# Attention and two feed-forward layers on one core: row factors applied to the softmax weights, not to the values and the output

## The chip, the cores and the metric

The kernel runs on one core of one Trainium2 chip. The metric is the device time of one execution in microseconds (us); smaller is better. Engines are named as in the profile: PE (TensorE, the matrix multiplier; PEld is its weight load), DVE (VectorE), ACT (ScalarE), POOL (GpSimd) and SP (SyncE, which here only issues DMA transfers).

## The reference, cut to what matters

```python
# B=4, H=8, S=576, D=64; all float32
scores = q @ k.T / sqrt(D); scores = where(causal, -1e9, scores)
a = exp(scores - scores.max(-1)); a /= a.sum(-1) + 1e-9
local = a @ v
q_p = phi(q)                       # where(q > 0, q, exp(q) - 1) + 1
mem_out = (q_p @ M_prev) / (q_p . z_prev + 1e-6)
g = 1 / (1 + exp(-beta))           # one number per head
attn = g * mem_out + (1 - g) * local
x = attn as (B*S, H*D)             # 2304 tokens of 512
x = (s * relu(x @ w_in)**2 + b) @ w_out          # d_ff = 2048
out = P(x @ w2_in) / Q(x @ w2_in) @ w2_out       # cubic over quadratic, d_ff = 2048
```

The weights of the two feed-forward layers come as 64-bit floats and are decoded on the chip into a high and a low part; the products are made of three matmuls each.

## The kernel before, in words

**Order of work.** All operations are first listed with their buffers, a cost for each engine that could do them (`ways`) and a due time; a list scheduler (`Plan.run`) then fixes the engine of each operation and the order on every engine, and the engines run these queues in order. Every plain load and store is issued by SP through one line, L364, in one in-order queue. A buffer that is reused comes from a ring (`at_ring(name, role, n, ...)`); a new user of a place waits for all users of the one before. RQ, RP, RT, RU and RV are the ring lengths of the queries and keys, the softmax weights, their transposes, one special transpose, and the values (`vm`).

**Attention.** There are 32 units: for each of 4 batches first the low rows (queries 0 to 383) and then the high rows (384 to 575), and in each of these four pairs of heads. A unit goes through these functions:

- `prepare_qk`, `prepare`: loads. Transposed queries `q` and keys `k` come as one transfer each and head (four a unit), values and the memory matrix as `vm` (ring of RV = 1), untransposed queries as `qm`.
- `scores`, `scores_last` (L610 to L679): score matmuls (L636, L670), masked row minimum on DVE (L643, L673), exponential on ACT (L654, L677) into the weight tiles `p` and `pu`, with row sums into `rs`.
- `sums` (L681): adds 1e-9 to `rs` (L690) and writes the reciprocals into `rec` (L693). For all but the first four units ("direct"), `rec` is then transposed on PE (L700, tile `ct`), copied to `c1`, written to DRAM (`crow`), and read back as a tile `cb` in which each row's reciprocal stands along the free axis of all 64 partitions of its head.
- `phi_a`, `phi_b`: the feature map of the queries, scaled by gate and norm (`c2`) and, in L721, by the row sum, so that the later multiplication by `cb` takes it out again; then transposed into `fs` (and `fl`). In the first four units `phi_b` also builds `cb`, by an expansion of `rec` into `rb`, three transposes and a copy.
- `split_v` (L587): the values of both heads times 1 - g (`omg`), into `vs`, two operations a unit, on whichever of ACT, DVE and POOL the scheduler picks.
- `transposes`, `transposes_last`: the weight tiles are transposed on PE (L504, L819) and copied into `th`.
- `values` (L832): products of `vs` and `th` (L848) and of the memory and `fs` (L856) into one PSUM tile `av`; DVE multiplies it by `cb` into `xp` (L859), which is stored.

**Around it.** While the units run, SP also loads the packed weights of the first half of layer one (tiles `dA...`), DVE, ACT and POOL decode them, and PE works on three narrow blocks of that half (`ha` L904, `acc` L977). When attention is done its memory is given to the second half's weights; wide blocks follow (`hw` and `aw`, then `hb`, `ab`, `hc`, `ac`).

Of the kernel before, what the change touches and what calls it, by code (L numbers as in the profile page):

```python
# [29 lines left out]
RQ, RP, RT, RU, RV = 3, 7, 8, 1, 1  # L30
# [224 lines left out]
def tile_kernel(ctx, tc, qk, vm, z, beta, w1i, w1o, s1, b1, w2i, w2o, a2, b2, out):  # L255
# [76 lines left out]
    cst.tile([P, 40], F32, name="fill_c")  # L332
# [4 lines left out]
    for n in ("rec0", "rec1", "qd0", "qd1"):  # L337
        plan.bufs[n].const = True
# [167 lines left out]
    def prepare_qk(p):  # L506
        u = units[p]
        r = u.r
        src = qk[u.b, u.hp].rearrange("p (j s) -> p j s", j=2)
        at_ring(f"q{p}", "q", RQ, [P, r.nq])  # L510
        at_ring(f"k{p}", "k", RQ, [P, r.nk])
        for j in range(2):
            m = slice(j * D, j * D + D)
            load(lambda m=m: g(f"q{p}")[m], lambda j=j, m=m: src[m, j, r.q0:r.q0 + r.nq], D * 4 * r.nq, (), ((f"q{p}", j),))
            load(lambda m=m: g(f"k{p}")[m], lambda j=j, m=m: src[m, j, SQ:SQ + r.nk], D * 4 * r.nk, (), ((f"k{p}", j),), p < 2)

    def diagonal(p):

        Q, QD = f"q{p}", f"qd{p % 2}"
# [67 lines left out]
    def split_v(p):  # L587

        hp, kb = units[p].hp, units[p].r.kb
        V, VS = f"vm{p}", f"vs{p}"  # L590
        at_ring(VS, "vs", 2, [P, kb, 2, D])
        for j in range(2):
            o = omg[:, 2 * hp + j:2 * hp + j + 1]

            def fn(e, j=j, o=o):
                src = g(V)[:, 0:kb].rearrange("p j (h d) -> p j h d", h=2)[:, :, j]
                if e is nc.scalar:
                    e.activation(g(VS)[:, :, j], src, AF.Copy, scale=o)
                else:
                    e.tensor_scalar(g(VS)[:, :, j], src, o, 0.0, ALU.mult, ALU.add)  # L600

            op(ways(kb * D, 0.09, 0.5, 0.5), fn, (V, "omg"), ((VS, j),), port=True)
# [7 lines left out]
    def scores(p):  # L610

        r = units[p].r
        Q, K, RS = f"q{p}", f"k{p}", f"rs{p}"
# [4 lines left out]
        for i, (cols, pieces) in enumerate(r.scores):  # L618
# [6 lines left out]
            for t, x, ka, kb, o in pieces:  # L625
# [55 lines left out]
    def sums(p):  # L681

        r = units[p].r
        RS, REC = f"rs{p}", f"rec{p % 2}"
        if r.tb == 4:
# [16 lines left out]
        copy(lambda: g(C1), lambda: g(CT)[0:nr, 0:P], P, (CT,), (C1,), act=-0.04)
        crow = dram.tile([2, r.nqt], F32, name=f"crow{p}")
        CR = f"crow{p}"
        buf(CR, None, obj=crow)
        if r.tb < NQ - 1:
            load(lambda: crow.rearrange("j (t q) -> (j t) q", q=P), lambda: g(C1), 1e4, (C1,), ((CR, 0),))
        else:
            load(lambda: crow[:, 0:P], lambda: g(C1)[0:2], 1e4, (C1,), ((CR, 0),))
            load(lambda: crow[:, P:P + 64].unsqueeze(0), lambda: g(C1)[2:3].rearrange("o (j q) -> o j q", j=2), 1e4, (C1,), ((CR, 1),))  # L710
        for j in range(2):
            load(lambda j=j: g(CB)[64 * j:64 * j + 64], lambda j=j: crow[j:j + 1, 0:r.nq].to_broadcast([64, r.nq]),
                 64 * 4 * r.nq, (CR,), ((CB, j),), late=LANDS_CB)

    def phi_b(p):

        r = units[p].r
        F, C, FS, PT, C1, CB, REC = (f"{x}{p}" for x in ("ph", "c2_", "fs", "pf", "c1_", "cb", "rec"))
        REC = f"rec{p % 2}"
        RS = f"rs{p}"  # L720
        small(lambda e: e.tensor_tensor(g(C), g(C), g(RS)[:, :, r.ta:r.tb + 1], ALU.mult), (RS, C), (C,))  # L721
# [6 lines left out]
        here = not r.direct or 2 * w <= 512
        RB = f"rb{p}"
        if r.direct:  # L730
            at_ring(RB, "xp", 2, [P, r.nt, P])
            copy(lambda: g(RB).rearrange("p t (h d) -> p h t d", h=2),
                 lambda: g(REC)[:, 0:2 * r.nt].rearrange("p (h t) -> p h t", h=2).unsqueeze(3).to_broadcast([P, 2, r.nt, D]),
                 r.nt * P, (REC,), (RB,), dve=0.5, pool=0.41)
# [11 lines left out]
        def along(dst, o1):  # L746

            for j in range(r.ta, r.tb + 1):
                flip(dst(), o1 + q0s[j] - r.q0, g(RB)[:, j - r.ta], j)

        def tr():
            phi_t()
            if r.direct and here:
                along(lambda: g(PT), w)

        pe(2 * r.nqt * (2 if r.direct and here else 1), tr, (F, RB) if r.direct and here else (F,), (PT,))
        if not r.direct:
            pass
        elif here:
            copy(lambda: g(CB), lambda: g(PT)[:, w:2 * w], w, (PT,), (CB,), act=-0.04)  # L760
        else:
            CT = f"ct{p}"
            bank(CT, free_banks(p))
            pe(2 * r.nqt, lambda: along(lambda: g(CT), 0), (RB,), (CT,))
            copy(lambda: g(CB), lambda: g(CT)[:, 0:w], w, (CT,), (CB,), act=-0.04)
# [66 lines left out]
    def values(p, runs):  # L832
# [3 lines left out]
        VS, FS, XP, AV, CB = (f"{x}{p}" for x in ("vs", "fs", "xp", "av", "cb"))  # L836
# [14 lines left out]
        pe(2 * sum(x[6] - x[5] for x in part) + 50 * len(part), mm, sorted({x[3] for x in part}) + [VS], (AV,))  # L851
# [7 lines left out]
        op(ways(w, None, 1.0), lambda e: e.tensor_tensor(g(XP), g(AV)[:, 0:w], g(CB), ALU.mult), (AV, CB), (XP,))  # L859
# [322 lines left out]
    for p in range(NPR):  # L1182
# [8 lines left out]
        events.append((t + 0.2, lambda p=p: split_v(p)))  # L1191
# [178 lines left out]
```

## Time and profile before

| | |
|---|---|
| median of 3 runs | 1040.17 us (1039.48 to 1042.01) |
| profiled execution, its own time | 1042.3 us |
| span of its instructions | 1040.5 us |
| PE, DVE, ACT, POOL busy, share of the span | 97%, 82%, 64%, 42% |
| mean granted TensorE clock | 0.988 of full speed |

A row of the view of stretches gives, for each stretch of time, the busy microseconds and the instructions of each engine, the granted clock of PE as a share of full speed, and the busy share of the DMA engines. The chain that ended last is followed back from the last instruction, at each step to what released it. In a row of the page or of a group, "dst<-src" are tile names without their numbers; a releaser is what ended an idle time.

### The profile page before, as it was taken

What the parts mean: (1) busy time and instruction counts of PE and PEld (TensorE: products, weight loads), DVE (VectorE), ACT (ScalarE), POOL (GpSimd) and SP (SyncE); (2) the same over time, 40 slices, a digit from 0 to 9 for tenths busy, and PEclk for the clock granted to TensorE, in tenths of its full rate; (3) what the DMA queues carried; (4) which work ended last, traced back from release to release, by engine and by line L of the source; (5) the groups of instructions that cost most, each with busy time, mean ns of one, the idle gap of its engine ahead of it and who ended that gap; (6) DMA issues with size and microseconds to landing.
All of it is one profiled execution on the core that took longest, in us unless ns stands there. A gap on an engine that the chain in (4) does not pass through costs nothing.

```text
span 1040.5 us, 16335 instructions
## 1 busy us (share of the span) xinstructions
PE 1008.0 (97%) x5396; PEld 835.2 (80%) x5396; DVE 854.5 (82%) x1470; ACT 668.9 (64%) x1415; POOL 439.3 (42%) x507
## 2 busy tenths in 40 slices
PE   6979989999999999999999999999999999999998
PEld 4557677887788886878878999888888888899997
DVE  6989889788849998999996444988888888888896
ACT  6967779677644544544444234777877776877886
POOL 3435433112101211212020004877776867867785
PEclk9989999999999999999999999999999999999999
DMA  6765676655423546676661235700100200100000
GB/s 190 229 206 168 191 229 208 175 162 151 117 61 126 181 139 227 209 243 196 226 211 37 89 102 149 246 0 21 59 1 1 72 1 1 36 28 1 31 1 31
DMA packets 76789, 123.58 MB, mean 119 GB/s; under 512 B 11832, under 2 KB 44704, under 8 KB 76704
## 3 DMA queue, kind: packets, MB, share of 16 engines
q1 hardware_dynamic: 72016, 113.74, 35.4%
q0 software_dynamic: 4224, 8.39, 2.6%
q8 instruction: 43, 0.70, 0.3%
q10 hardware_dynamic: 464, 0.40, 0.2%
q14 instruction: 42, 0.34, 0.1%
HBM read 95.17 MB, written 27.32 MB: 118 GB/s over the span
## 4 chain that ended last, share of the span: by engine, by line
PE 72%; DVE 13%; DMA 7%; ACT 4%; issue 2%; SPq 1%; POOL 0%; ACTq 0%; DVEq 0%; POOLq 0%
PE hc L904 19%; PE ac L1139 19%; PE ab L1053 5%; PE hb L904 5%; PE hw L904 5%; PE aw L1016 4%; PE av L848 3%; PE ha L904 3%; PE s L636 3%; PE acc L977 2%; PE pt L504 2%; ACT p L654 1%; SPq L364 1%; DMA vm<-in_vm 1%; DMA k<-in_qk 1%
## 5 line engine op out<-in xcount | busy, mean ns | idle before, releaser
L1118 DVE RECIPROCAL qe<-qe 128x512 f32<-128x512 f32 (+2 forms) x82 | 242.6, 2959 | 49.2 <-POOL qe L380 49.2
L904 PE MATMUL hc<-xc_h,w2ih 128*128 128x512 f32 (+1 forms) x320 | 117.9, 368 | 0.0
L904 PE MATMUL hc<-xc_h,w2il 128*128 128x512 f32 (+1 forms) x320 | 117.8, 368 | 0.0
L904 PE MATMUL hc<-xc_l,w2ih 128*128 128x512 f32 (+1 forms) x320 | 117.7, 368 | 0.0
L380 POOL TENSOR_TENSOR qe<-qe,qb 128x512 f32<-128x512 f32 (+2 forms) x82 | 94.9, 1157 | 52.5 <-ACT qb L1103 51.4
L1139 PE MATMUL ac<-w2oh,ghc 128*128 128x512 f32 x288 | 112.6, 391 | 0.0
L1139 PE MATMUL ac<-w2ol,ghc 128*128 128x512 f32 x288 | 112.5, 391 | 0.0
L1139 PE MATMUL ac<-w2oh,glc 128*128 128x512 f32 x288 | 112.3, 390 | 0.0
L380 POOL TENSOR_TENSOR glc<-po,ghc 128x512 fp32r<-128x512 f32 (+2 forms) x82 | 95.0, 1158 | 23.3 <-ACT ghc L370 23.1
L380 POOL TENSOR_TENSOR pm<-pm,s 128x512 f32<-128x512 f32 (+2 forms) x82 | 95.6, 1166 | 18.7 <-ACT pm L1103 17.8
L1109 ACT ACTIVATE s<-hc 128x512 f32<-128x512 f32 (+2 forms) x82 | 44.7, 546 | 63.1 <-PE hc L904 60.2
L654 ACT ACTIVATE p<-s,st 128x128 f32<-128x128 f32 (+3 forms) x128 | 66.9, 531 | 19.1 <-DVE st L643 17.9
L1103 ACT ACTIVATE pm<-hc,prm 128x512 f32<-128x512 f32 (+2 forms) x82 | 59.7, 727 | 24.4 <-DVE hc L1120 24.0
L504 PE MATMUL pt<-ident,p 128*128 128x128 f32 x320 | 58.6, 280 | 9.6 <-ACT th L370 4.8
L904 PEld LDWEIGHTS hc<-xc_h,w2il 128*128 128x128 f32 x320 | 60.1, 188 | 8.8 <-DVE po L1122 0.3
L904 PEld LDWEIGHTS hc<-xc_l,w2ih 128*128 128x128 f32 x320 | 60.1, 188 | 8.6
L904 PEld LDWEIGHTS hc<-xc_h,w2ih 128*128 128x128 f32 x320 | 60.1, 188 | 7.6
L1103 ACT ACTIVATE qb<-s,cq,b1abs 128x512 f32<-128x512 f32 (+2 forms) x82 | 62.7, 764 | 2.1 <-POOL qe L380 2.1
L643 DVE CUSTOM_DVE_ANT_0 s<-s,mask 128x128 f32<-128x128 f32 (+3 forms) x128 | 60.5, 508 | 4.3 <-PE s L636 2.9
L1139 PEld LDWEIGHTS ac<-w2oh,ghc 128*128 128x128 f32 x288 | 54.0, 188 | 11.4
L1139 PEld LDWEIGHTS ac<-w2oh,glc 128*128 128x128 f32 x288 | 54.1, 188 | 11.0 <-POOL glc L380 0.6
L1139 PEld LDWEIGHTS ac<-w2ol,ghc 128*128 128x128 f32 x288 | 54.1, 188 | 10.5
(488 smaller groups left out, 2844.1 us busy)
## 6 DMA issues: line engine op xcount, KB each, us to landing
vm<-in_vm SPq DMA_DIRECT2D x16, 384.0 KB
k<-in_qk SPq DMA_DIRECT2D x32, 144.0 KB
out_y<-ob SPq DMA_DIRECT2D x18, 256.0 KB
qm<-in_vm SPq DMA_DIRECT2D x16, 256.0 KB
w2d<-sh SPq DMA_DIRECT2D x16, 256.0 KB
w2d<-sl SPq DMA_DIRECT2D x16, 256.0 KB
w2oh<-w2d POOLq DMA_DIRECT2D x4, 1024.0 KB, 16.9
w2ol<-w2d POOLq DMA_DIRECT2D x4, 1024.0 KB, 18.5
```

The costliest lines, as they stand in the source:

```text
L380: op(ways(c, None, dve, pool), lambda e: e.tensor_tensor(dst(), x(), y(), alu), r, w, port=True)
L504: nc.tensor.transpose(dst[:, o:o + P], src, ident)
L636: nc.tensor.matmul(g(b)[:, o2:o2 + kb - ka], g(Q)[m, q], g(K)[m, ka:kb], start=True, stop=True)
L643: e.tensor_tensor_reduce(sp, sp, mask[:, m0:m0 + kb - ka], -scale, 3.0e38 if x == 0 else st[:, t:t + 1], ALU.add, ALU.min, st[:, t + x:t + ...
L654: e.activation(g(f"p{n}_{i}")[:, o:o + kb - ka], g(b)[:, o2:o2 + kb - ka], AF.Exp, scale=-1.0, bias=g(f"st{n}")[:, z_:z_ + 1], accum_out=g ...
L904: nc.tensor.matmul(hs(), m, y, start=c == 0 and k == 0, stop=c == KC - 1 and k == 2)
L1016: nc.tensor.matmul(g(ACC)[:, 0:w], outp(y, f)[:, cs], g(z_), start=f == 0 and k == 0, stop=f == HF - 1 and k == 2)
L1053: nc.tensor.matmul(g(ACC)[:, 0:w], outp(y, f)[:, cs], g(z_), start=f == 0 and k == 0, stop=f == HF - 1 and k == 2)
L1103: return lambda e: e.activation(g(dst)[:, ks], g(src)[:, ks], AF.Identity, scale=m, bias=b)
L1109: op(ways(c, -0.04), lambda e, ks=ks: e.activation(g(S2)[:, ks], g(HS)[:, ks], AF.Square), (HS,), part(S2))
L1118: op({"DVE": 0.07 + c * 0.00625}, lambda e, ks=ks: e.reciprocal(g(QE)[:, ks], g(QE)[:, ks]), part(QE), part(QE))
L1139: nc.tensor.matmul(g(ACC), g(x_)[:, ks], g(f"w2o{y}{i}")[:, o], start=f == 0 and q == 0, stop=f == NF - 1 and q == 2)
```

## The change: what it does

The row factor (1 - g) / (sum + 1e-9) is computed in place in `rs`, and each weight tile is multiplied by it, row block by row block, before it is transposed: a new helper `scaled` in `sums`, six operations in a low unit and three in a high one, each on ACT, DVE or POOL. The values are used straight from `vm`; `vs`, `rec`, `ct`, `c1`, `crow`, `cb` and `rb` go, with L721. `xp` becomes a copy that ACT or DVE can make. Queries and keys of a head come in one transfer into one tile `qk`; in the high units this takes the 64 columns between them along. RP goes from 7 to 9 and RV from 1 to 3. `gates` makes a small table `omg2` for the high units, three more short DVE copies.

```diff
-RQ, RP, RT, RU, RV = 3, 7, 8, 1, 1
+RQ, RP, RT, RU, RV = 3, 9, 8, 1, 3
...
-        at_ring(f"q{p}", "q", RQ, [P, r.nq])
-        at_ring(f"k{p}", "k", RQ, [P, r.nk])
+        w = r.ko + r.nk
+        at_ring(f"qk{p}", "q", RQ, [P, w])
         for j in range(2):
             m = slice(j * D, j * D + D)
-            load(lambda m=m: g(f"q{p}")[m], ... ((f"q{p}", j),))
-            load(lambda m=m: g(f"k{p}")[m], ... ((f"k{p}", j),), p < 2)
+            load(dst, rows_, D * 4 * w, (), ((f"qk{p}", j),), p < 2 and j == 1)
...
-    def split_v(p):
-        at_ring(VS, "vs", 2, [P, kb, 2, D])
-        for j in range(2):
-            ...
-            op(ways(kb * D, 0.09, 0.5, 0.5), fn, (V, "omg"), ((VS, j),), port=True)
+    def split_m(p):
...
-        small(lambda e: e.reciprocal(g(REC)[:, 0:2 * r.nt].rearrange(by, h=2), g(RS)[:, :, ts]),
-              (RS,), (REC,), ("DVE",))
-        if r.direct:
-            return
-        pe(2 * P, lambda: nc.tensor.transpose(g(CT)[:, 0:P], g(REC), ident), (REC,), (CT,))
-        copy(lambda: g(C1), lambda: g(CT)[0:nr, 0:P], P, (CT,), (C1,), act=-0.04)
-        ... one or two loads C1 -> crow, two loads crow -> CB
+        small(lambda e: e.reciprocal(g(RS)[:, :, ts], g(RS)[:, :, ts]), (RS,), (RS,), ("DVE",))
+        small(lambda e: e.tensor_tensor(
+            g(RS)[:, :, ts], g(RS)[:, :, ts], omg2[:, 2 * hp:2 * hp + 2] if r.tb == 4
+            else omg[:, 2 * hp:2 * hp + 2].unsqueeze(2).to_broadcast([P, 2, r.nt]), ALU.mult), (RS, "omg", "omg2"), (RS,))
+
+        def scaled(name, part, a, b, c):
+            def fn(e):
+                x = g(name)[:, a:b]
+                if e is nc.scalar:
+                    e.activation(x, x, AF.Copy, scale=g(RS)[:, c[0], c[1]:c[1] + 1])
+                else:
+                    e.tensor_scalar(x, x, g(RS)[:, c[0], c[1]:c[1] + 1], 0.0, ALU.mult, ALU.add)
+
+            op(ways(b - a, 0.09, 0.5, 0.41), fn, ((name, part) if part is not None else name, RS),
+               ((name, part) if part is not None else name,), port=True)
+
+        for i, (cols, pieces) in enumerate(r.scores):
+            for t, x, ka, kb, o in pieces:
+                for j in range(2):
+                    scaled(f"p{2 * p + j}_{i}", t, o, o + kb - ka, (j, t))
+        if r.tb == 4:
+            scaled(f"pu{p}", None, 0, S, (0, 4))
...
-        small(lambda e: e.tensor_tensor(g(C), g(C), g(RS)[:, :, r.ta:r.tb + 1], ALU.mult), (RS, C), (C,))
...
-            copy(lambda: g(RB)..., lambda: g(REC)..., r.nt * P, (REC,), (RB,), dve=0.5, pool=0.41)
-            pe(2 * r.nqt, lambda: along(lambda: g(CT), 0), (RB,), (CT,))
-            copy(lambda: g(CB), lambda: g(CT)[:, 0:w], w, (CT,), (CB,), act=-0.04)
...
-                nc.tensor.matmul(g(AV)[64 * j:64 * j + 64, ra:rb], g(VS)[:, kb, j], g(TH)[:, o:o + rb - ra],
+                nc.tensor.matmul(g(AV)[64 * j:64 * j + 64, ra:rb], g(V)[:, kb, D * j:D * j + D], g(TH)[:, o:o + rb - ra],
...
-        op(ways(w, None, 1.0), lambda e: e.tensor_tensor(g(XP), g(AV)[:, 0:w], g(CB), ALU.mult), (AV, CB), (XP,))
+        copy(lambda: g(XP), lambda: g(AV)[:, 0:w], w, (AV,), (XP,), act=-0.04)
```

## Rows read from the trace of the kernel before

**Rows 1.** Stretches of the span: busy us of PE, PEld, DVE, ACT, POOL; clock, DMA.
```profile
0.00:16.00 16.00, 7.50 (x38) 6.13 (x38) 7.75 (x39) 6.96 (x22) 3.97 (x17) 1.00 0.68 212
16.00:160.00 144.00, 129.64 (x877) 93.65 (x878) 128.25 (x393) 113.24 (x329) 59.58 (x115) 0.93 0.69 202
60.00:80.00 20.00, 14.93 (x83) 10.35 (x85) 15.16 (x51) 13.15 (x42) 7.88 (x15) 0.69 0.69 211
160.00:304.00 144.00, 142.66 (x1114) 115.19 (x1115) 116.05 (x389) 99.86 (x292) 30.28 (x76) 1.00 0.52 150
304.00:1040.00 736.00, 728.16 (x3373) 620.20 (x3368) 602.46 (x652) 448.86 (x774) 345.44 (x299) 1.00 0.29 95
```

**Rows 2.** The chain that ended last, 0 to 160 us, shares by line.
```profile
by line: DMA vm<-in_vm 6.6%; DMA k<-in_qk 6.6%; SPq L364 6.0%; DMA qm<-in_vm 5.1%; PE s L636 5.0%; ACT p L654 4.9%; DMA q<-in_qk 4.7%; PE pt L504 3.9%; PE av L848 3.7%; PE ha L904 3.5%; DVE s L643 3.4%; issue 3.3%; DMA dAo2r<-in_w1o 3.3%; D
```

**Rows 3.** The same chain, 160 to 304 us.
```profile
by line: PE acc L977 15.4%; PE av L848 15.1%; PE ha L904 14.9%; PE s L636 12.6%; PE pt L504 11.5%; PE su L670 5.7%; PE av L856 5.6%; ACT p L654 3.8%; PE pf L504 2.6%; PE pt L819 2.3%; PE ct L700 1.6%; DVE s L643 1.4%; DMA qm<-in_vm 1.3%; is
```

**Rows 4.** Pieces of the chain in order of time: start, length, what.
```profile
70.50 5.83 DMA vm<-in_vm
...
81.86 1.81 PE ha L904 x15
...
104.63 0.33 PE pf L504 x3
```

**Rows 5.** DMA issues on SP's queue (L364) up to 305 us: min/median/max ns of an issue.
```profile
L364 SPq DMA_DIRECT2D q<-in_qk x64: 465/549/1625, 0.7 to 264.5; - x64
L364 SPq DMA_DIRECT2D k<-in_qk x60: 465/588/1107, 4.6 to 267.1; - x60
L364 SPq DMA_DIRECT2D cb<-crow x56: 444/588/2330, 51.6 to 303.6; - x56
L364 SPq DMA_DIRECT2D crow<-c x44: 244/302/661, 47.1 to 299.9; - x44
```

**Rows 6.** Waits of POOL up to 305 us: total, times, longest.
```profile
POOL vs L600 <- DMA vm<-in_vm: 43.2, 12, 9.4
```

**Rows 7.** Operations that go: engine, operation, count: min/median/max ns.
```profile
L600 POOL TENSOR_SCALAR vs<-vm,omg x23: 425/495/897, 9.2 to 233.6; 128x192 f32<-128x192 f32 x14, 128x320 f32<-128x320 f32 x9
L600 DVE TENSOR_SCALAR vs<-vm,omg x17: 339/419/1051, 9.1 to 290.1; 128x320 f32<-128x320 f32 x9, 128x192 f32<-128x192 f32 x8
L598 ACT ACTIVATE vs<-vm,omg x24: 442/560/564, 23.8 to 290.1; 128x320 f32<-128x320 f32 x14, 128x192 f32<-128x192 f32 x10
L370 ACT COPY c<-ct x15: 238/250/256, 49.2 to 299.3; 4x128 f32<-4x128 f32 x8, 6x128 f32<-6x128 f32 x7
```

**Rows 8.** Groups by shape up to 305 us: busy us, mean ns; idle before.
```profile
L572 DVE TENSOR_SCALAR qm<-qm 128x384 f32<-128x384 f32 x5 | 1.8, 360 | 0.5 <-ACT ph L566 0.3
L572 DVE TENSOR_SCALAR qm<-qm 128x256 f32<-128x256 f32 x3 | 0.9, 288 | 0.0
L570 ACT ACTIVATE qm<-qm,ones 128x384 f32<-128x384 f32 x3 | 1.9, 633 | 0.0
L570 ACT ACTIVATE qm<-qm,ones 128x256 f32<-128x256 f32 x7 | 3.6, 518 | 0.1
L574 POOL TENSOR_SCALAR qm<-qm 128x384 f32<-128x384 f32 x8 | 4.1, 511 | 10.9 <-ACT ph L566 8.3 <-issue 1.7 <-DMA xTd<-xp 0.7
L574 POOL TENSOR_SCALAR qm<-qm 128x256 f32<-128x256 f32 x6 | 2.4, 405 | 15.5 <-ACT ph L566 6.5 <-DMA qm<-in_vm 5.1 <-DMA q<-in_qk 3.7
L859 DVE TENSOR_TENSOR xp<-av,cb 128x384 f32<-128x384 f32 x16 | 8.8, 549 | 0.7 <-PE pt L504 0.6
L370 ACT COPY th<-pt 128x384 f32<-128x384 f32 x98 | 44.5, 489 | 3.1 <-PE pt L504 3.0
```

**Rows 9.** The transposes of the reciprocals on PE, and the first unit's start.
```profile
L700 PE MATMUL ct<-ident,rec 128*128 128x128 f32 x28 | 8.4, 300 | 0.6 <-ACT p L654 0.3 <-ACT th L370 0.3
...
11.09 1.02 PE L504 MATMUL pt<-ident,p 128*128 128x128 f32 x6 [0.27 <-POOL qm L574]
...
14.34 0.17 DVE L690 TENSOR_SCALAR rs<-rs 128x6 f32<-128x6 f32 x1
```

More of the change, by code (lines that the diff above doesn't have):

```diff
@@ L308, in tile_kernel @@
         nc.gpsimd.affine_select(m, m, pattern=[[-1, 64]], compare_op=ALU.is_ge, fill=-2.0e9 / scale, base=0, channel_multiplier=1)
-    for n in ("rec0", "rec1", "qd0", "qd1"):
+    for n in ("qd0", "qd1"):
         t = at.tile([P, P], F32, name=n)
@@ L331, in tile_kernel @@
     omg = cst.tile([P, H], F32, name="omg")
-    cst.tile([P, 40], F32, name="fill_c")
+    omg2 = cst.tile([P, H, 2], F32, name="omg2")
+    buf("omg2", None, obj=omg2)
+    cst.tile([P, 24], F32, name="fill_c")
     buf("gate", None, obj=gate)
@@ L336, in tile_kernel @@
     buf("sb", None, obj=sb)
-    for n in ("rec0", "rec1", "qd0", "qd1"):
+    for n in ("qd0", "qd1"):
         plan.bufs[n].const = True
@@ L398, in gates @@
         op(ways(H, None, 1.0), lambda e: e.tensor_copy(gate2[:, :, 0], gate), ("gate",), (("gate2", 0),))
+        op(ways(H, None, 1.0), lambda e: e.tensor_copy(omg2[:, :, 0], omg), ("omg",), (("omg2", 0),))
+        for j in range(2):
+            m = slice(64 * j, 64 * j + 64)
+            op(ways(H, None, 1.0), lambda e, j=j, m=m: e.tensor_copy(
+                omg2[m, :, 1].rearrange("p (a h) -> p a h", h=2), omg[m, j::2].unsqueeze(2).to_broadcast([64, NP, 2])),
+               ("omg",), (("omg2", 1 + j),))
         for j in range(2):
@@ L478, in tile_kernel @@
         r.nqt = r.nt * P
+        r.ko = r.nk if r.ta == 0 else SQ - r.q0
         r.where = {t: (i, o) for i, (_, pieces) in enumerate(r.scores) for t, x, _, _, o in pieces if x == 0}
@@ L509, in prepare_qk, with dst, rows_ @@
         src = qk[u.b, u.hp].rearrange("p (j s) -> p j s", j=2)
-        at_ring(f"q{p}", "q", RQ, [P, r.nq])
-        at_ring(f"k{p}", "k", RQ, [P, r.nk])
+        w = r.ko + r.nk
+        at_ring(f"qk{p}", "q", RQ, [P, w])
         for j in range(2):
             m = slice(j * D, j * D + D)
-            load(lambda m=m: g(f"q{p}")[m], lambda j=j, m=m: src[m, j, r.q0:r.q0 + r.nq], D * 4 * r.nq, (), ((f"q{p}", j),))
-            load(lambda m=m: g(f"k{p}")[m], lambda j=j, m=m: src[m, j, SQ:SQ + r.nk], D * 4 * r.nk, (), ((f"k{p}", j),), p < 2)
+            def dst(m=m):
+                return g(f"qk{p}")[m].rearrange("p (x s) -> p x s", x=2) if r.ta == 0 else g(f"qk{p}")[m]
+            def rows_(m=m, j=j):
+                if r.ta:
+                    return src[m, j, r.q0:r.q0 + w]
+                two = qk[u.b, u.hp][m, (2 * S if j else 0):(2 * S if j else 0) + 2 * SQ].rearrange("p (x s) -> p x s", x=2)
+                o = j * (SQ - S)
+                return two[:, :, o:o + r.nk]
+            load(dst, rows_, D * 4 * w, (), ((f"qk{p}", j),), p < 2 and j == 1)
     def diagonal(p):
-        Q, QD = f"q{p}", f"qd{p % 2}"
+        Q, QD = f"qk{p}", f"qd{p % 2}"
         for j in range(2):
@@ L585, in phi_a @@
             if units[p].r.tb < NQ - 1 else gate2[:, 2 * hp:2 * hp + 2], ALU.mult), (C, "gate", "gate2"), (C,))
-    def split_v(p):
-        hp, kb = units[p].hp, units[p].r.kb
-        V, VS = f"vm{p}", f"vs{p}"
-        at_ring(VS, "vs", 2, [P, kb, 2, D])
-        for j in range(2):
[L593 to L600, printed above, removed]
-            op(ways(kb * D, 0.09, 0.5, 0.5), fn, (V, "omg"), ((VS, j),), port=True)
+    def split_m(p):
         if units[p].r.split_m:
@@ L612, in scores @@
         r = units[p].r
-        Q, K, RS = f"q{p}", f"k{p}", f"rs{p}"
+        QK, RS = f"qk{p}", f"rs{p}"
         ns = (2 * p, 2 * p + 1)
@@ L635, in mm @@
                         m = slice(D * j, D * j + D)
-                        nc.tensor.matmul(g(b)[:, o2:o2 + kb - ka], g(Q)[m, q], g(K)[m, ka:kb], start=True, stop=True)
-                pe(4.9 * (kb - ka), mm, (Q, K), [(b, t) for b in banks], 7)
+                        nc.tensor.matmul(g(b)[:, o2:o2 + kb - ka], g(QK)[m, q], g(QK)[m, r.ko + ka:r.ko + kb], start=True, stop=True)
+                pe(4.9 * (kb - ka), mm, (QK,), [(b, t) for b in banks], 7)
                 for n, b in zip(ns, banks):
@@ L659, in scores_last @@
     def scores_last(p):
-        Q, K, RS, ST, PR = f"qd{p % 2}", f"k{p}", f"rs{p}", f"su{p}", f"pu{p}"
+        Q, K, RS, ST, PR = f"qd{p % 2}", f"qk{p}", f"rs{p}", f"su{p}", f"pu{p}"
         at_ring(ST, "su", 2, [P, 2])
@@ L666, in scores_last @@
             bank(SB, free_banks(p))
-            ks = slice(x * QB, x * QB + QB)
+            ks = slice(units[p].r.ko + x * QB, units[p].r.ko + x * QB + QB)
             def mm(SB=SB, ks=ks):
@@ L683, in sums @@
         r = units[p].r
-        RS, REC = f"rs{p}", f"rec{p % 2}"
+        RS, hp = f"rs{p}", units[p].hp
         if r.tb == 4:
@@ L690, in sums @@
         small(lambda e: e.tensor_scalar(g(RS)[:, :, ts], g(RS)[:, :, ts], 1e-9, None, ALU.add), (RS,), (RS,))
-        by = "p (h t) -> p h t" if r.tb < NQ - 1 else "p (t h) -> p h t"
-        small(lambda e: e.reciprocal(g(REC)[:, 0:2 * r.nt].rearrange(by, h=2), g(RS)[:, :, ts]),
-              (RS,), (REC,), ("DVE",))
-        if r.direct:
-            return
-        CT, C1, CB, nr = f"ct{p}", f"c1_{p}", f"cb{p}", 2 * r.nqt // P
-        at_ring(CB, "cb", 2, [P, r.nq])
-        bank(CT, free_banks(p))
@@ L700, in sums @@
-        pe(2 * P, lambda: nc.tensor.transpose(g(CT)[:, 0:P], g(REC), ident), (REC,), (CT,))
-        at_ring(C1, "c1", 2, [nr, P])
-        copy(lambda: g(C1), lambda: g(CT)[0:nr, 0:P], P, (CT,), (C1,), act=-0.04)
[L703 to L710, printed above, removed]
@@ L711, in sums @@
-        for j in range(2):
-            load(lambda j=j: g(CB)[64 * j:64 * j + 64], lambda j=j: crow[j:j + 1, 0:r.nq].to_broadcast([64, r.nq]),
-                 64 * 4 * r.nq, (CR,), ((CB, j),), late=LANDS_CB)
+        small(lambda e: e.reciprocal(g(RS)[:, :, ts], g(RS)[:, :, ts]), (RS,), (RS,), ("DVE",))
+        small(lambda e: e.tensor_tensor(
+            g(RS)[:, :, ts], g(RS)[:, :, ts], omg2[:, 2 * hp:2 * hp + 2] if r.tb == 4
+            else omg[:, 2 * hp:2 * hp + 2].unsqueeze(2).to_broadcast([P, 2, r.nt]), ALU.mult), (RS, "omg", "omg2"), (RS,))
@@ L715, in phi_b @@
+        for i, (cols, pieces) in enumerate(r.scores):
+            for t, x, ka, kb, o in pieces:
+                for j in range(2):
+                    scaled(f"p{2 * p + j}_{i}", t, o, o + kb - ka, (j, t))
+        if r.tb == 4:
+            scaled(f"pu{p}", None, 0, S, (0, 4))
     def phi_b(p):
         r = units[p].r
-        F, C, FS, PT, C1, CB, REC = (f"{x}{p}" for x in ("ph", "c2_", "fs", "pf", "c1_", "cb", "rec"))
-        REC = f"rec{p % 2}"
-        RS = f"rs{p}"
-        small(lambda e: e.tensor_tensor(g(C), g(C), g(RS)[:, :, r.ta:r.tb + 1], ALU.mult), (RS, C), (C,))
+        F, C, FS, PT = (f"{x}{p}" for x in ("ph", "c2_", "fs", "pf"))
@@ L724, in phi_b @@
         at_ring(FS, "fs", 2, [P, r.nq], F32R if r.split_m else F32)
-        if r.direct:
-            at_ring(CB, "cb", 2, [P, r.nq])
         w = r.nq
[L728 to L734, printed above, removed]
         bank(PT, free_banks(p))
@@ L744, in phi_t @@
                 nc.tensor.matmul(g(PT)[:, P:P + 64], g(F)[:, 1], both, start=True, stop=True)
[L746 to L763, printed above, removed]
-            pe(2 * r.nqt, lambda: along(lambda: g(CT), 0), (RB,), (CT,))
-            copy(lambda: g(CB), lambda: g(CT)[:, 0:w], w, (CT,), (CB,), act=-0.04)
+        pe(2 * r.nqt, phi_t, (F,), (PT,))
         copy(lambda: g(FS), lambda: g(PT)[:, 0:w], w, (PT,), (FS,), act=-0.04)
@@ L835, in values @@
         r = u.r
-        VS, FS, XP, AV, CB = (f"{x}{p}" for x in ("vs", "fs", "xp", "av", "cb"))
+        V, FS, XP, AV = (f"{x}{p}" for x in ("vm", "fs", "xp", "av"))
         MB = memory_in(p)
@@ L847, in mm @@
                 _, j, kb, TH, o, ra, rb = x
-                nc.tensor.matmul(g(AV)[64 * j:64 * j + 64, ra:rb], g(VS)[:, kb, j], g(TH)[:, o:o + rb - ra],
+                nc.tensor.matmul(g(AV)[64 * j:64 * j + 64, ra:rb], g(V)[:, kb, D * j:D * j + D], g(TH)[:, o:o + rb - ra],
                                  start=x in firsts, stop=False, skip_group_check=True)
-        pe(2 * sum(x[6] - x[5] for x in part) + 50 * len(part), mm, sorted({x[3] for x in part}) + [VS], (AV,))
+        pe(2 * sum(x[6] - x[5] for x in part) + 50 * len(part), mm, sorted({x[3] for x in part}) + [V], (AV,))
         def mem():
@@ L1190, in tile_kernel @@
         events.append((t + 0.1, lambda p=p: phi_a(p)))
-        events.append((t + 0.2, lambda p=p: split_v(p)))
+        events.append((t + 0.2, lambda p=p: split_m(p)))
         events.append((t + PHB * d, lambda p=p: phi_b(p)))
```

## The prediction, made before the change was run

> **What bounds the kernel now.** I read the stretches first: which engine is full, and when. After 304 us PE is busy 728.16 of 736 us [rows 1]; nothing there is edited, so that part can only start earlier or later, and what counts is the time at which attention ends. Before that there are two regimes. From 160 to 304 us PE is busy 142.66 of 144 us, and the chain there runs through PE lines almost alone: a bound of matrix work [rows 1, 3]. From 16 to 160 us no engine is full: PE 129.64, DVE 128.25, ACT 113.24 of 144 us, and PE's weight loads fill only 93.65 against 115.19 in the later stretch of the same length [rows 1]. Loads per us are a truer measure than busy time, whose ends are modelled: at the later density, 115.19 of 144 or 0.80, the early work would take 117 us. So up to 27 us of PE's time are lost there, and the next ceiling is DVE with 128.25.
>
> The chain of the first 160 us says to what. A share of 1% is 1.6 us there: transfers of `vm` 10.6 us, of keys 10.6, of queries 7.5, of `qm` 8.2, and SP's issuing itself 9.6 [rows 2]. One such piece, the 5.83 us wait for `vm` from 70.5 us, stands in the stretch where PE's granted clock is 0.69, that is partly the lower of its two levels, after PE had run short of work [rows 1, 4].
>
> **The change, part by part.** Lengths are those of the profiled execution, 1042.3 us with a span of 1040.5.
>
> *The values' ring.* Today a load of `vm` waits until the unit before has scaled its values, and the scaling waits for the load: POOL alone stood 43.2 us behind such loads [rows 6]. With three places and no scaling, the values are first needed by the products, about a unit later. Between 0 and 10.6 us of chain can go [rows 2]. The high units' memory matrix comes in the same transfer, and `qm` and the decoders' loads stand in the same queue as before and are late next, so I take half: -5.3.
>
> *SP's queue.* All 56 loads of `cb` and 44 stores of `crow` go, and 62 of the 124 loads of queries and keys on SP [rows 5]. By medians that is 33 + 13 + 35 = 81 us of issuing in an in-order queue; each `cb` issue also waited there for its `crow` to land, with every later load behind it (up to 2.33 us for one issue). The chain holds 9.6 us of issuing; these 162 issues, with 62 that stay in the same four groups and about 200 others on that queue, are near 4 of 10, so -3.6 (bounds 0 and -9.6) [rows 2, 5].
>
> *Queries and keys in one transfer.* The bytes stay (in high units 832 columns for 768), the ring stays at three. Their 18.1 us of chain are mostly flight [rows 2]; bounds 0 and -18.1, and I take -2, near the lower end, because only the second issue disappears.
>
> *Transposes of reciprocals.* 28 on PE, 300 ns each by the records, but neighbours start 0.11 us apart (three in 0.33) [rows 4, 9]. The 16 in the PE-bound part give -1.8; the chain says 1.6% of 144, -2.3, as the other bound [rows 3]. The 12 early ones, and the 12 for the first four units, lie where PE has room: 0. The memory product and the weights' transposes are unchanged.
>
> *Scaling moves from values to weights.* Gone: 23 on POOL, 17 on DVE, 24 on ACT, 11.4 + 7.1 + 13.4 = 31.9 us, and 28 copies of `ct`, 7.0 us at the 250 ns of the 15 on ACT [rows 7]. The first four units lose 8 copies of 384 columns, 8 x 0.489 = 3.9 by the row of `th` [rows 8]. Together 42.8 us. New: 16 low units x 2 heads x (128 + 256 + 384 columns), 16 high units x (2 x 512 + 576). By the two shapes of the nearest rows, in-place scalings of `qm`, and a straight line through them: DVE 0.216, 0.288, 0.360, 0.432, 0.468, total 49.0 us; ACT 0.403 to 0.806, total 86.6; POOL 0.299 to 0.670, total 69.3 [rows 8]. The scheduler spread the old scaling over all three, so I take the mean, 68.3: net +25.5 us (bounds +6.2 and +43.8), half of it early. Over three engines of 144 us that is 12.8 of 432, 3.0%, at most 4.3 us if all three were the limit. They are not, POOL is 59.58 of 144 [rows 1]: +2, bounds 0 and +4.3. In these ranges DVE stays near where it was, since `xp` (549 ns on DVE) may now be copied by ACT (489 for the same shape) [rows 8]; L721 goes and one small product with `omg` comes, zero.
>
> [...] The rows give DVE 72 ns for 128 more columns and about 144 ns before the first [rows 8]. [...]
>
> *The new wait.* A transpose now needs all exponentials of the unit, three small operations on `rs`, and its scaling. In the later part PE has narrow-block matmuls to put in between: 0. At the start it has none: the first transposes ran at 11.09 us, before the first sums were taken at 14.34 [rows 9]. They now wait at least until after those, about 3 us; the copies behind them were late anyway, so +2 (bounds 0 and +3.3).
>
> *Clock.* From 16 to 160 us the granted share is 0.93, 10 us of full-speed PE time; the piece at 60 to 80 us alone is 6.2 of it [rows 1]. With `vm` there in time part comes back, but PE is not the limit: -1.5 (bounds 0 and -10).
>
> Sum: -5.3 - 3.6 - 2 - 1.8 + 2 + 2 - 1.5 = -10.2. From 1042.3 this gives 1032.1 for an execution like the profiled one, and from the median, which lies 2.1 below it, **1030 us**. It keeps below the ceiling: DVE's 128.25 of 144 us would allow 15.7.
>
> **Rivals.**
>
> *All waits go (1018 us).* If the early part becomes DVE-bound, with `xp` moved to ACT (half of 16 x 0.549 and as many shorter ones, some 7 us off DVE), 144 falls to about 123 us; with -1.8 later and +2 at the start, -21. For it: transfers and issuing hold 46 us of that chain [rows 2]. Against it: three engines at 80 to 90% rarely mesh, and DMA is already busy 0.69 [rows 1].
>
> *The transfers are hidden anyway (1038 us).* If `qm`, the decoders' loads and DVE simply become the last to arrive, only PE's -1.8 is left with a rest of the clock. For it: the waits of `vm` end mostly on POOL, which has room [rows 1, 6]. Against it: the 5.83 us piece has nothing else beside it on the chain [rows 4].
>
> *Weights come late to PE (1046 us, slower).* PE's queue is in order. If the scaling of a unit is placed on POOL or ACT behind an operation that itself waits, the transposes stand and every matmul behind them too, scores of the next unit included. Place: 16 to 82 us, before the long run of `ha` begins [rows 4], some seven units of 9 us (32 in 288 us). Price: three small operations at 0.17 and one round of scaling at 1.7 on DVE, 2.2 us a unit, 16 us if nothing hides it, against -10: +6 [rows 8, 9]. It decides once the scaling ends later than the next unit's scores; the longer `p` ring (9 places, a low unit takes 4) lets these go ahead, which speaks against it. For it: POOL's records show operations held for many us by one wait [rows 6].
>
> **How the numbers follow.** About 0.3%, 3 us, is what a measurement of this kernel can tell from no change. Chances: forecast (1024 to 1035) 0.42; all waits go (1012 to 1024) 0.18; hidden anyway (1035 to 1043) 0.20, of which two thirds within 0.3%; late weights (1043 to 1058) 0.20. Faster is 0.42 + 0.18 + 0.07 = 0.67, the same 0.13, slower 0.20. The range 1014 to 1046 leaves out the far ends of both outer cases, about 0.2; the likeliest case alone has 1024 to 1035.
>
> **What would show it.** Right: no `vm` in the chain of the first 160 us, SP's share under half of 6%, weight loads per us up in that part, the clock near 1.00 at 60 to 80 us, `hw` beginning some 10 us earlier, and the stretch after it as long as now. Wrong: PE waiting at L504 for scaled `p`, ACT or DVE above 95% in the early part, a chain that still holds keys and `qm` for as long, or a later part that grows by what the early one gave.

## The result and the profile after

The changed kernel takes 1029.84 us (median of 6 runs, 1027.63 to 1031.87) against 1041.34 us for the kernel before in the same session. The ratio is 0.9892, interval 0.9871 to 0.9914: 11.2 us faster, by 9.0 to 13.4. The forecast was 1030 and a step of 10.2 us.

The stretches of the changed kernel, columns as in [rows 1] (busy us of PE, PEld, DVE, ACT, POOL with their instructions, granted clock, DMA share, GB/s); attention ends about 9 us earlier, so the early part is shown twice, to 150 and to 160 us:

```profile
16.00:150.00 134.00, 125.07 (x853) 90.71 (x853) 130.27 (x404) 117.56 (x331) 53.91 (x100) 0.96 0.71 201
60.00:80.00 20.00, 17.94 (x123) 14.47 (x122) 17.39 (x52) 14.25 (x42) 8.79 (x15) 0.83 0.72 207
16.00:160.00 144.00, 133.71 (x923) 98.06 (x923) 139.48 (x433) 125.87 (x356) 58.97 (x110) 0.96 0.71 199
```

In the same 144 us PE loads weights for 98.06 us, before 93.65 [rows 1]: more matrix work gets done. DVE went from 128.25 to 139.48 us, and to 150 us it is busy 130.27 of 134, which is 97%. The clock rose from 0.93 to 0.96, and from 0.69 to 0.83 between 60 and 80 us.

The chain that ended last, 0 to 160 us, shares by line:

```profile
by line: DVE s L648 11.2%; issue 5.9%; DMA qm<-in_vm 4.7%; DVE su L678 3.9%; DVE ph L596 3.5%; PE ha L877 3.4%; DVE c L598 3.0%; DVE p L707 2.9%; SPq L366 2.9%; DMA qk<-in_qk 2.8%; DVE tz L382 2.6%; DVE fl L743 2.4%; DMA prm<-in_a 2.3%; DVE
```

Where [rows 2] had `vm`, keys, SP's issuing, `qm` and queries, 29% together, there is now mostly a list of DVE lines; `qm` stays, with 4.7%. `vm` is not among the lines shown, the transfers of queries and keys fell from 11.3% to 2.8%, SP's issuing from 6.0% to 2.9%. This chain is that of one execution and moves with the order of the work: in the run with another order, whose time is the same, `qm` has 9.1%, `qk` 6.3% and the largest DVE line 8.8%.

SP's own queue (now L366) up to 300 us, for [rows 5]: min/median/max ns of an issue, and the count:

```profile
L366 SPq DMA_DIRECT2D qk<-in_qk x62: 465/600/1637, 0.7 to 256.3; - x62
```

The merged transfer costs one issue of 600 ns where there were two of 549 and 588. The waits of SP's own queue up to 300 us, added up over the whole view, are 84 us before and 181 us in the change: SP has time to spare where it had little. The scaling by engine and shape up to 300 us (busy us, mean ns | idle before), for the forecast's prices from [rows 8]:

```profile
L705 ACT ACTIVATE p<-p,rs 128x512 f32<-128x512 f32 x18 | 12.8, 726 | 8.7 <-DVE rs L697 7.1 <-POOL rs L697 1.6
...
L707 DVE TENSOR_SCALAR p<-p,rs 128x512 f32<-128x512 f32 x11 | 6.3, 576 | 0.1
...
L707 DVE TENSOR_SCALAR pu<-pu,rs 128x576 f32<-128x576 f32 x12 | 6.2, 514 | 0.0
...
L707 DVE TENSOR_SCALAR p<-p,rs 128x256 f32<-128x256 f32 x16 | 5.1, 352 | 0.0
L707 DVE TENSOR_SCALAR p<-p,rs 128x384 f32<-128x384 f32 x13 | 5.1, 410 | 0.0
...
L707 DVE TENSOR_SCALAR p<-p,rs 128x128 f32<-128x128 f32 x14 | 3.6, 283 | 0.1
```

On ACT 512 columns took 726 ns, the forecast's line gave 748. On DVE every width is dearer than its line: 283, 352, 410, 576 and 514 ns for 216, 288, 360, 432 and 468. DVE took 66 of the 144 operations, 26 us of 71.

Behind attention, the start of `hw` (the first wide block) and of `hc`, a later one (one row of each; the last columns are first and last start). Before:

```profile
L904 PE MATMUL hw<-xw_h,w1ilA x96: 389/389/628, 301.8 to 434.6; 128*128 128x512 f32 x96
L904 PEld LDWEIGHTS hc<-xc_h,w2il x320: 186/188/188, 638.9 to 1021.6; 128*128 128x128 f32 x160
```

After:

```profile
L877 PE MATMUL hw<-xw_h,w1ilA x96: 389/389/474, 292.8 to 421.8; 128*128 128x512 f32 x96
L877 PEld LDWEIGHTS hc<-xc_h,w2il x320: 186/188/188, 627.9 to 1010.6; 128*128 128x128 f32 x160
```

`hw` begins 9.0 us earlier, `hc` 11.0, the span ends 10.4 earlier. Attention's gain is carried to the end.

### The profile page after: what moved, and what is told of

Its sections match the earlier page's. It is cut to its first block, busy times and chain, and to the rows that moved or that the text cites. A ratio compares the mean times of both kernels' runs of the same rounds, so it can differ in the third digit from the quotient of the medians.

```text
span 1030.1 us, 15977 instructions
## 1 busy us (share of the span) xinstructions
PE 1001.4 (97%) x5356; PEld 829.1 (80%) x5356; DVE 866.3 (84%) x1528; ACT 676.8 (66%) x1425; POOL 437.3 (42%) x484
## 4 chain that ended last, share of the span: by engine, by line
PE 69%; DVE 22%; issue 3%; DMA 2%; ACT 2%; SPq 1%; POOL 0%; DVEq 0%; ACTq 0%; POOLq 0%
PE hc L877 19%; PE ac L1112 19%; PE ab L1026 7%; PE hb L877 6%; PE hw L877 3%; PE ha L877 2%; PE av L821 2%; PE acc L950 2%; DVE s L648 2%; PE aw L989 2%; PE pt L513 2%; PE s L641 2%; DVE hw L893 1%; PE av L829 1%; DVE glw L902 1%
## 5 line engine op out<-in xcount | busy, mean ns | idle before, releaser
L382 POOL TENSOR_TENSOR qe<-qe,qb 128x512 f32<-128x512 f32 (+2 forms) x82 | 94.9, 1157 | 52.4 <-ACT qb L1076 51.4
L382 POOL TENSOR_TENSOR glc<-po,ghc 128x512 fp32r<-128x512 f32 (+2 forms) x82 | 94.9, 1158 | 23.3 <-ACT ghc L372 23.1
L382 POOL TENSOR_TENSOR pm<-pm,s 128x512 f32<-128x512 f32 (+2 forms) x82 | 95.5, 1165 | 18.7 <-ACT pm L1076 17.8
L659 ACT ACTIVATE p<-s,st 128x128 f32<-128x128 f32 (+3 forms) x128 | 67.3, 537 | 18.4 <-DVE st L648 15.7
L513 PE MATMUL pt<-ident,p 128*128 128x128 f32 x320 | 60.5, 287 | 7.5 <-ACT p L659 2.1
L1112 PEld LDWEIGHTS ac<-w2oh,ghc 128*128 128x128 f32 x288 | 54.0, 188 | 11.3
```

What stands on the lines that cost most here:

```text
L382: op(ways(c, None, dve, pool), lambda e: e.tensor_tensor(dst(), x(), y(), alu), r, w, port=True)
L513: nc.tensor.transpose(dst[:, o:o + P], src, ident)
L659: e.activation(g(f"p{n}_{i}")[:, o:o + kb - ka], g(b)[:, o2:o2 + kb - ka], AF.Exp, scale=-1.0, bias=g(f"st{n}")[:, z_:z_ + 1], accum_out=g ...
L1112: nc.tensor.matmul(g(ACC), g(x_)[:, ks], g(f"w2o{y}{i}")[:, o], start=f == 0 and q == 0, stop=f == NF - 1 and q == 2)
```

## The experiments

Theory A: transfers came late, because of SP's queue and the values' single place, and the gain is that they no longer do. Theory B: transfers were hidden, and the gain is the removed work (transposes of reciprocals, small copies, the product with `cb`). Theory C, formed after the first profile: with the transfers in time, DVE bounds the early part, so the new scaling takes back part of the gain. All runs are compared with the kernel before on the same chip in the same session.

| run | ratio | interval | us against before |
|---|---|---|---|
| the change | 0.9892 | 0.9871 to 0.9914 | -11.2 |
| before, values' ring 3 | 1.0003 | 0.9989 to 1.0017 | +0.3 |
| before, merged loads | 0.9960 | 0.9948 to 0.9972 | -4.2 |
| before, merged loads and ring 3 | 0.9922 | 0.9907 to 0.9937 | -8.1 |
| changed, old traffic put back | 0.9946 | 0.9927 to 0.9966 | -5.6 |
| changed, two loads a head | 0.9942 | 0.9928 to 0.9956 | -6.0 |
| changed, other order | 0.9909 | 0.9894 to 0.9924 | -9.5 |
| changed, values' ring 2 | 0.9914 | 0.9899 to 0.9930 | -9.0 |
| changed, weights' ring 7 | 0.9912 | 0.9897 to 0.9927 | -9.2 |
| changed, no scaling | 0.9843 | 0.9827 to 0.9858 | -16.3 |
| changed, scaling on ACT and POOL | 0.9846 | 0.9831 to 0.9860 | -16.0 |
| the same, and `ph` on POOL | 0.9862 | 0.9845 to 0.9880 | -14.4 |
| changed, scaling on DVE | 1.0001 | 0.9988 to 1.0015 | +0.1 |

The last column is the ratio's distance from 1 times 1041 us. The ratio is not that of the two medians, which can put a run up to 1.3 us elsewhere: the merged loads alone are 5.4 us faster by the medians, 4.2 by the ratio.

**The values' ring alone.**

```diff
-RQ, RP, RT, RU, RV = 3, 7, 8, 1, 1
+RQ, RP, RT, RU, RV = 3, 7, 8, 1, 3
```

> The kernel before with nothing changed but the ring of the values, 1 to 3. Theory A (transfers came late): the waits for vm, 10.6 us of the early chain, go in part, 1035 us or less (-5 or more), and the early part's chain holds no vm. Theory B (the gain is removed work on PE and in copies, transfers were hidden): within 2 us of 1041.

1039.86 us, no difference: theory B's number, not theory A's. Yet the waits it aims at did go. POOL's waits of this run, for `vm` (before in [rows 6]) and for a free place of `vs`, and its early chain (0 to 160 us):

```profile
POOL vs L600 <- DMA vm<-in_vm: 8.4, 2, 6.3
POOL vs L600 <- PE av L848: 20.7, 10, 4.3
```

```profile
by line: issue 7.5%; DMA qm<-in_vm 7.1%; DMA xa0r<-xTd 6.5%; DMA k<-in_qk 5.7%; DVE s L643 5.6%; ACT p L654 5.2%; SPq L364 3.9%; PE s L636 3.7%; PE av L848 3.5%; DMA dAo5r<-in_w1o 3.5%; DMA q<-in_qk 3.2%; ACT th L370 2.3%; DVE su L673 2.0%;
```

43.2 us of waiting became 8.4, `vm` left the chain, and other transfers of the same queue stand there in its place: `qm` 7.1%, `xa0r` 6.5%, keys, `dAo5r`. A wait was removed and the next one behind it took over. Part of POOL's waiting only changed its reason: the scaled values `vs` have two places of their own, which this run left as they were, and the wait for the products (`av`) that free one rose from 5.3 us to 20.7. So theory A fails in its first form, in which the values' single place cost time by itself; whether SP's queue was late is not decided here.

**Merged loads alone, and with the ring.** The edit of the change to `prepare_qk` (and the names that follow from it) in the kernel before; the second run has RV = 3 too.

> The kernel before with one transfer for the queries and keys of a head and nothing else. Theory A: 62 fewer issues on SP, 35 of its some 190 us of issuing, and less waiting for keys: 1038 us (-2 to -5). Theory B: within 2 us of 1041.

> The kernel before with the merged transfers and the values' ring of three, no other part of the change. Theory A: with SP relieved the earlier values now count as well, 1030 to 1033 us, most of the whole gain. If the ring is worth nothing even then, 1035 as with the merged transfers alone, and the rest of the gain is the transfers of the reciprocals.

1034.10 and 1033.73 us, against 1039.53 and 1041.62 for the kernel before in their sessions: -4.2 us alone, -8.1 with the ring by the ratios, -5.4 and -7.9 by the medians. These two parts without any scaling edit are over two thirds of the whole gain. Theory B has no place for that. That the ring, worth nothing while SP was late, is worth something once SP is not (3.9 us by the ratios, 2.5 by the medians) is likely but not shown: the two intervals only just do not meet, the order alone moves the time by some 2 us (below), and the two profiled executions have the same span, 1032.1 and 1032.0 us. Nor did `vm` leave the early chain: it has 9.9% with the merged loads, 5.2% with the ring too.

**Put back into the changed kernel: the traffic, the two loads.**

```diff
+        if not r.direct:
+            op({"POOL": 0.2}, lambda e: e.memset(g(f"c1_{p}"), 0.0), (RS,), (f"c1_{p}",))
+            ... c1 -> crow, crow -> cb on SP as before; nothing reads cb
```

> The changed kernel with the transfers of the reciprocals put back: the same stores to DRAM and broadcast loads on SP, of a small tile that POOL fills with zeros, and nobody reads what they bring. Theory A: SP's 46 us of issuing and its waits for the stores to land are back, 1034 to 1038 us (+4 to +8). Theory B: 1030 to 1032, the traffic was hidden.

1032.59 us: 5.6 us slower than the change, or 3.9 against the run with another order, which shared its session. That is theory A's range or just below it; the median itself lies between the two theories' ranges. 28 small fills on POOL are in it, and `cb` has a ring of one place where the kernel before had two.

```diff
-            load(dst, rows_, D * 4 * w, (), ((f"qk{p}", j),), p < 2 and j == 1)
+            load(... [m, 0:r.nq], src[m, j, r.q0:r.q0 + r.nq], ...)
+            load(... [m, r.ko:r.ko + r.nk], src[m, j, SQ:SQ + r.nk], ..., p < 2)
```

> The changed kernel with queries and keys of a head in two transfers again, into the same tile. Theory A, as the first runs left it (SP's queue of issues is what was late, the ring of the values alone is worth nothing): the 62 issues come back, 1033 to 1035 us (+4). Theory B (removed work): 1030, no difference beyond 2 us.

1035.54 us, 5.2 us slower than the change: the 62 issues cost about as much here as they did in the kernel before. In the form in which SP's queue was late, theory A holds from both sides. The waits of SP's own queue, added up as above, go along with the issues: 84 us before, 87 with the ring alone, 129 with the merged loads, 181 in the change, 140 with two loads a head, 124 with the old traffic. The runs take away or put back issues and transfers together, so which of the two costs the time is not separated.

Theory B, which wanted no difference, falls as the whole account, but not as a part of it. If the measured parts may be added up, the merged loads with the ring (-8.1), the traffic (-3.9 to -5.6) and the price of the scaling (below, +5.1) make -6.9 to -8.6 us. The 2.6 to 4.3 us that are left of 11.2 may be the removed work, which no run tried by itself, or parts that do not simply add up.

**How much the order alone moves.**

```diff
-TIMES = 8.5, 8.0, 1.2
+TIMES = 8.5, 8.1, 1.2
```

> A measure of how much the order alone moves the time: the changed kernel with all due times of units shifted by 0.1 us, the same work, so that the scheduler makes a somewhat different order. Both theories: within 3 us of 1030. If it moves more, differences of that size in the other runs say nothing about their edits.

1029.44 us; by ratios 1.7 us from the change, within the intervals. Differences under some 2 us between two runs here say nothing about their edits, and this rests on one other order only.

**The two rings in the changed kernel.** RV = 2 in one run, RP = 7 in the other.

> The changed kernel with two places for the values instead of three; they are held now until the products. If the load of the next but one unit then comes late: 1033 to 1040, with vm back among the waits of PE or of the copies of the memory matrix. If two do: 1029 to 1032.

> The changed kernel with seven places for the weight tiles instead of nine. If the weights' longer life needs them (they wait for sums, scaling and transposes): 1033 to 1038, with ACT waiting to write p. If the seven do: 1029 to 1032.

1031.94 and 1031.64 us, -9.0 and -9.2 against before: the same as the change within that noise. The third place for the values and the two added weight tiles buy nothing that can be measured.

**The price of the scaling.**

```diff
-                    scaled(f"p{2 * p + j}_{i}", t, o, o + kb - ka, (j, t))
+                    pass
 ...
-            scaled(f"pu{p}", None, 0, S, (0, 4))
+            pass
```

> The changed kernel without the multiplications of the weights by their rows' factors, so that the attention part is left unnormalised; everything else, the sums and the factors themselves included, stays. It prices the scaling: 144 operations, 71 us of engine time in the profile of the changed kernel, 26 of it on DVE. Theory C (the early part is now bound by DVE, 130 of 134 us): 13 us of DVE's early work goes and the time falls by 5 to 10 us, 1020 to 1025. If the scaling hides beside other work, as in the forecast's sum, 1026 to 1029 (-1 to -4).

1025.01 us: the scaling costs 5.1 us, at the low end of theory C's range and above the forecast's +2. The early stretch, without scaling:

```profile
16.00:150.00 134.00, 127.32 (x917) 95.21 (x917) 127.92 (x402) 108.97 (x315) 49.42 (x97) 0.97 0.75 216
```

DVE is nearly as full as in the change, 127.92 of 134 us, but PE loads weights for 95.21 us in place of 90.71: DVE did other work in that time, and more of PE's work got done.

**Where the scaling runs.** Same work on other engines: DVE barred in the first run, DVE alone in the last.

```diff
-            op(ways(b - a, 0.09, 0.5, 0.41), fn, ...
+            op(ways(b - a, 0.09, None, 0.41), fn, ...    # ACT and POOL
+            op(ways(b - a, None, 0.5, None), fn, ...     # the other run: DVE
```

> The changed kernel with the scaling allowed on ACT and POOL only. Theory C: DVE loses 26 us of work, ACT and POOL take it; faster by 2 to 6 us, 1024 to 1028, if ACT (118 of 134 us early) doesn't fill up. Rival: ACT becomes the limit or weights come late to PE, 1030 to 1036.

> The changed kernel with all of the scaling on DVE. Theory C (DVE bounds the early part): by the rows of the changed kernel, 283 to 576 ns by width, some 57 us on DVE in place of 26, half of it early, so 8 to 15 us slower: 1038 to 1045, as slow as before the change. Rival (DVE's share is only a symptom, and what helped off DVE was another order): within 4 us of 1030.

Without DVE 1025.75 us, as fast as with no scaling at all, and faster than both kernels. On DVE alone 1040.04 us: the whole gain of the change is gone. The early stretch of the first and then of the second:

```profile
16.00:150.00 134.00, 124.02 (x899) 91.70 (x898) 127.88 (x399) 125.24 (x356) 71.70 (x126) 0.97 0.72 209
```

```profile
16.00:150.00 134.00, 120.62 (x797) 83.98 (x796) 132.27 (x413) 105.61 (x302) 49.08 (x92) 0.94 0.65 194
```

With scaling on DVE, DVE is full (132.27 of 134 us), ACT is busy for only 105.61 us and PE's weight loads drop to 83.98 from 90.71. With DVE barred, ACT (125.24) and POOL (71.70) take it, PE loads 91.70, `hw` begins at 285.5 us, 7.3 before the change's, and the span ends 5.3 us earlier. That the scaling costs what it takes of DVE is shown by this pair; an accident of order would not give 16 us between them.

Where it costs is less clear than theory C has it. With all of it on DVE the loss is early. With DVE barred PE's loads rise by only 1.0 us up to 150 us; more of the rise, 1.5 us, comes from 150 to 290 us, where DVE was not full, 122.23 of 140 us. First the change, then the run with DVE barred:

```profile
150.00:290.00 140.00, 136.74 (x1059) 109.93 (x1060) 122.23 (x422) 103.70 (x294) 30.80 (x64) 1.00 0.49 136
150.00:290.00 140.00, 136.85 (x1052) 111.38 (x1054) 104.17 (x364) 107.99 (x296) 43.33 (x85) 1.00 0.46 133
```

**A candidate beyond that.** The product of the feature map with its factors, too, barred from DVE:

```diff
-                lambda: g(C).unsqueeze(3).to_broadcast([P, 2, r.nt, D]), ALU.mult, r.nt * P, (F, C), (F,), pool=0.8)
+                lambda: g(C).unsqueeze(3).to_broadcast([P, 2, r.nt, D]), ALU.mult, r.nt * P, (F, C), (F,), dve=None, pool=0.8)
```

> A candidate: the scaling on ACT and POOL only, and the product of the feature map with its factors (a line of phi_b, so far on DVE or POOL) on POOL only. DVE loses some 8 us more before 300 us. Theory C: 1022 to 1025 us. If ACT (125 of 134 us early without DVE's help) or POOL's late results are the next bound: 1026 to 1032.

1026.22 us, no better than the run with the scaling off DVE; the intervals overlap. Theory C's 1022 to 1025 is missed, the other range met. Its early chain (0 to 160 us):

```profile
by line: ACT p L659 10.5%; DVE s L648 7.6%; DMA qm<-in_vm 5.6%; ACT p L705 4.9%; issue 4.9%; ACT th L372 4.5%; PE ha L877 3.2%; PE pt L513 3.1%; DMA prm<-in_b 2.8%; PE av L821 2.8%; PE s L641 2.5%; SPq L366 2.3%; DVE su L678 1.8%; ACT pu L6
```

ACT, with the exponentials (L659) and its scaling (L705), has come up beside DVE. That moving more work off one of the two now reaches the other is read from this chain and not shown.

## Why the prediction was right, step by step

The time (1030 for 1029.84), the sign and the mechanism held: the early, transfer-bound part got shorter, the rest moved with it. Several terms were off and made each other up, so that it came within 0.2 us is luck.

*Values' ring, -5.3.* Alone nothing; with the merged loads 2.5 to 3.9 us, which is hardly more than the order's 2. The forecast named what would be late next, `qm` and the decoders' loads, and still took half of the wait as gain. A wait on the chain is not a gain while the transfers behind it come from the same late queue, or while the next buffer (`vs`) has no free place.

*SP's queue, -3.6.* The mechanism was right, the size too small. Putting the traffic of the reciprocals back cost 3.9 to 5.6 us, and the term also held the 62 issues of the merged loads: together with the next term it stands at -5.6, and the two edits measured 8 to 11 us if they may be added. What the forecast named beside the issuing itself, that each `cb` issue held the queue until its `crow` had landed, is not borne out: 2.33 us is the length of one issue, and in the kernel before SP's queue waited for `crow` twice up to 305 us, 1.4 us in total:

```profile
SPq L364 <- DMA crow<-c: 1.4, 2, 0.8
```

*One transfer for queries and keys, -2.* Measured 4.2 in the kernel before and 5.2 in the changed one: sized at under half. "Only the second issue disappears" was true, and that was worth more than it seemed: 62 issues, each with its transfer, in a queue on whose head everything else waits.

*Scaling, +2.* Measured 5.1, a little above the term's own bound of 4.3. The engine time was nearly right: 71 us for 68.3, of it 26.3 on DVE, where DVE's line, read from 8 records, gives 22.7. What failed was to spread it over three engines. "DVE stays near where it was" did not hold: it went from 128.25 to 139.48 of 144 us, with 66 of the 144 operations, and time taken from DVE cost more than time taken from ACT and POOL. The mark "DVE above 95% in the early part" was listed as a sign against the forecast; it came true without the time going wrong, and is no sign by itself: with no scaling at all DVE is still at 95%.

*Transposes, -1.8; first unit, +2.* Not tried by themselves. The first transposes did move, from 11.09 to 15.20 us, behind the first sums:

```profile
13.73 0.23 POOL L695 TENSOR_SCALAR rs<-rs 128x6 f32<-128x6 f32 x1
...
15.20 0.30 PE L513 MATMUL pt<-ident,p 128*128 128x128 f32 x1 [1.06 <-ACT p L659]
```

*Clock, -1.5.* It rose less than marked (0.83 between 60 and 80 us, not near 1.00). In the kernel before, stretches of 0.5 us between 54 and 82 us show two levels, 1.00 and 0.50, and steps between them: 0.50 from 61 to 64 us, after PE had been busy only 1.90 of 4 us (56.5 to 60.5), and from 71.5 to 81 us, after 0.00 of 1 us (68 to 69). That the one brings the other is not shown, and the clock's worth was not measured apart.

*The rivals.* "Hidden anyway" fell with the two runs that put issues back. "Late weights" did not come: up to 300 us PE waits for ACT's `p` at its transposes only 2.1 us (and 2.6 for its weight loads behind POOL's scaling), and seven weight tiles do as well as nine. "All waits go", 1018 us, had its condition met, an early part bound by DVE with `xp` on ACT, but not its time: it took DVE's work as 7 us less, and the scaling made it more. With the scaling off DVE the time is 1025.75 us, some 4 of the 12 us from 1030 to 1018.

## What to carry to other kernels

In an in-order issue queue that is late, count issues, each with its transfer, and not bytes alone: merging 62 pairs, with the same bytes or slightly more, was worth 4 to 5 us, and a longer ring for one tensor was worth nothing while the queue was late. After removing waits, ask which engine is full next, and keep new work off it; here the same multiplications cost 5 us where the scheduler put them, nothing that could be measured without DVE, and 16 us on DVE alone. Before taking part of a wait as gain, look at what stands behind it in the same queue.

## What had not been expected of the hardware

On DVE 512 columns took longer (576 ns in the mean) than 576 columns (514). The mean is of two kinds: in the changed kernel ten of the eleven operations took 0.47 to 0.51 us and one, which began 0.08 us into an operation of POOL, 1.49. The run with all scaling on DVE has more of them, 3 of 32 at 1.36 to 1.50 us, all three begun inside an operation of POOL. From its records, first a quiet one, then two operations of which the first began beside one of POOL (start, length, engine, what):

```profile
53.37 0.47 DVE L707 TENSOR_SCALAR p<-p,rs 128x512 f32<-128x512 f32 x1
...
118.58 1.27 POOL L382 TENSOR_TENSOR w1ilA<-dAi_1f,w1ihA 128x512 fp32r<-128x512 f32 x1
...
118.78 1.75 DVE L707 TENSOR_SCALAR p<-p,rs 128x512 f32<-128x512 f32 x2
```

Alone an operation takes 0.47 us. The pair that starts at 118.78, in the middle of POOL's operation, takes 1.75, where two quiet ones in a row take 0.86 to 0.88 by other records of that run: some 0.9 us more, and POOL's operation still had 1.07 us to go. In all four cases POOL's operation is a difference of two 128x512 tiles (L382) that takes 1.27 to 1.45 us; of the quiet ones in the changed kernel two began inside shorter operations of POOL and took 0.48 us (at 111.72) and 0.51 (at 131.58). So not every operation of POOL goes with a long one on DVE, and what ties the two is not shown. A price read from calm records leaves this out. It explains little of the scaling's 5.1 us for 2, though: the one long operation of the changed kernel is 1 us, and it comes after 270 us. The quiet ones, too, are dearer than DVE's line, 0.48 us for 0.432 and 0.51 for 0.468; why is open.
